# Two transfers of 64 rows for each output tile in place of one transfer over both batch halves

## The chip, the cores and the metric

The kernel runs on one core of a Trainium2 chip. The metric is the device time of one execution in microseconds (us); the time before is the median of three runs. A profile of one execution comes with it: for every instruction on every engine its start and duration, and for the 16 DMA engines of the core the packets that they moved. TensorE is PE in the rows, VectorE DVE, ScalarE ACT, GpSimd POOL and SyncE SP. "SPq" is the queue of SyncE, on which the transfers of this kernel are issued.

## What is computed

A decayed linear attention over 4 batches, 8 heads and 768 positions, then two feed-forward blocks without residuals over the 3072 tokens:

```python
for t in range(S):
    state = gamma[None, :, None, None] * state + np.einsum('bhd,bhe->bhde', k[:, :, t], v[:, :, t])
    y[:, :, t] = scale * np.einsum('bhd,bhde->bhe', q[:, :, t], state)
x = np.ascontiguousarray(y.transpose(0, 2, 1, 3)).reshape(B * S, H * D)   # 3072 x 512
# first block: 512 -> 1024 -> 512
h = x @ w_in; sm = softmax(h); solu = h * sm
x = (layernorm(solu) * g_ln) @ w_out
# second block: 512 -> 2048 -> 512
h = x @ w_in2
out = (h * np.cos(h)) @ w_out2
...
```

The output is 3072 x 512 in float32, with the rows ordered by batch and then by position.

## The kernel before

The attention works in 24 steps. A step takes 64 consecutive positions of two batches at once (`steps` holds pairs of batch pair `bp` and position block `i`), so the 128 rows that it yields are 64 rows of one batch followed by 64 rows of the next. The first feed-forward block follows on groups of two such steps, and its result goes to DRAM and comes back through `load_y`, for the second block.

The second block runs in six passes over 512 tokens (four steps of the attention each; the loop over `n` near the end of `body`). In each pass `up(n, j)` makes one of 16 slices of the hidden layer: 12 matmuls on PE (line 362), then the cosine and the split into a high and a low part on ACT and DVE. `down(n, j)` multiplies such a slice into four accumulators in PSUM, one for each tile of 128 tokens: 12 matmuls (line 387). `down` lags `up` by three slices. In the last pass the last three slices of `down` are run tile by tile, so that the four tiles end one after the other.

After the last slice of a tile, `down` copies the accumulator into a tile `o` in SBUF of 128 rows x 512 columns (four buffers), the left half on ACT and the right half on DVE (line 392), and issues the store to the output in DRAM on SP's queue (line 394). Row p of `o` belongs to batch `2*bp` for p below 64 and to batch `2*bp + 1` from 64 on. In DRAM the two halves lie 768 rows apart, and each of them is one unbroken stretch of 64 rows of 2 KB. The store before writes both halves in one transfer, whose target has three dimensions, 2 x 64 x 512:

```python
bp, i = steps[4 * n + t]
nc.sync.dma_start(
    out=out.rearrange("(p b s) f -> p b s f", b=2, s=S)[bp, :, i * C:(i + 1) * C], in_=o)
```

The order of PE's work is that of the program. The order on the other engines and on SP's queue is made by a planner from its own estimate of times. SP issues transfers in the order of its queue; before that, it waits for what the transfer needs. `load_y` for the next pass shares this queue: it reads four blocks of 128 x 512 (`yt`, line 350, two buffers), which ACT and DVE split into `yh` and `yl` (lines 120 and 123) for the next `up`. Other transfers that the prediction speaks of are in the attention's loads: `load_step` brings `X` and `W` in halves of 64 rows (lines 91, 92, 94 and 95, 128 KB each) and `kn` whole (line 96, 256 KB). `mm2` stores the first block's result in whole tiles of 128 rows (`y1d<-ys`, line 342, 256 KB). The program ends with waits of SP for the outstanding transfers and a barrier of all engines (line 629).

Of the kernel before, what the change touches and what calls it, by code (L numbers as in the profile page):

```python
# [21 lines left out]
B, H, S, D = 4, 8, 768, 64  # L22
C = 64
# [27 lines left out]
def body(ctx: ExitStack, tc: tile.TileContext, qx, kt, kn, vn, c_sc, c_mg,  # L51
         w_in1, w_out1, gln, w_in2, w_out2, out):
    nc = tc.nc
# [7 lines left out]

    y1d = [dram.tile([128, KD, 512], F32, name=f"y1d{n}") for n in range(NBLK)]

    # ---- phase 1 pools
    ph1 = ExitStack()
    p_w1 = ctx.enter_context(tc.tile_pool(name="w1", bufs=1, side="left", reuse_waits="tile"))
    p_u = ctx.enter_context(tc.tile_pool(name="u", bufs=2 * EARLY + 2, side="left", reuse_waits="tile"))
# [6 lines left out]
    pa = att.enter_context(tc.tile_pool(name="att", bufs=3, side="right", reuse_waits="tile"))  # L74
    psa = att.enter_context(tc.tile_pool(name="psa", bufs=1, side="right", space=PSUM))

    # ---- loads of a step of the attention
    steps = [(bp, i) for bp in range(NB2) for i in range(NI)]
    st = {}

# [30 lines left out]
    ident = const.tile([128, 128], F32, name="ident")  # L111
    make_identity(nc, ident)

    # ---- weights, each as a high and a low part
    w1h = p_w1.tile([128, KD, FF1], F32R, tag="w1h", name="w1h")
    w1l = p_w1.tile([128, KD, FF1], F32R, tag="w1l", name="w1l")
    o1 = []
# [87 lines left out]
        else:  # L205
            split(w2h[c][:, k], w2l[c][:, k], load_w(w_in2[k * 128:(k + 1) * 128, c * 1024:(c + 1) * 1024]))

    # ---- attention
    s_ps = [None]

    def att_prep(n):
# [49 lines left out]
            in1=d["mg"][:, 1].unsqueeze(2).to_broadcast([128, NHP, 2, C]), op=ALU.mult)  # L261
        xs[n] = x32

    # ---- first block
    lns = {}

    def split_x(n):
# [73 lines left out]
            nc.scalar.activation(out=ys, in_=y1, func=AF.Copy)  # L341
            nc.sync.dma_start(out=y1d[g // 2][:, 2 * p:2 * p + 2, (g % 2) * 256:(g % 2) * 256 + 256], in_=ys)

    # ---- second block
    def load_y(n):
        yh = p2["sb"].tile([128, KD, 512], F32R, tag="yh", name="yh")
        yl = p2["sb"].tile([128, KD, 512], F32R, tag="yl", name="yl")
        for k in range(KD):
            t = p2["sb"].tile([128, 512], F32, tag="yt", name="yt", bufs=2)
            nc.sync.dma_start(out=t, in_=y1d[n][:, k])  # L350
            split(yh[:, k], yl[:, k], t)
        p2["y", n] = (yh, yl)
# [25 lines left out]
    def down(n, j, tiles=range(4)):  # L378
        gh, gl = p2["g", n, j]
        wh, wl = p2["o", j]  # L380
        if ("acc", n) not in p2:
            p2["acc", n] = [p2["psacc"].tile([128, 512], F32, tag=f"acc{t}", name=f"acc{t}") for t in range(4)]
        for t in tiles:
            acc = p2["acc", n][t]
            ts_ = slice(t * 128, t * 128 + 128)
            for m, (a, w) in enumerate(((gh, wh), (gl, wh), (gh, wl))):
                nc.tensor.matmul(out=acc, lhsT=a[:, ts_], rhs=w, start=(j == 0 and m == 0),  # L387
                                 stop=(j == K2 - 1 and m == 2))
            if j == K2 - 1:
                o = p2["wo"].tile([128, DM], F32, tag="o", name="o", bufs=4)  # L390
                for c, eng in enumerate((nc.scalar.copy, nc.vector.tensor_copy)):
                    eng(o[:, c * 256:c * 256 + 256], acc[:, c * 256:c * 256 + 256])
                bp, i = steps[4 * n + t]
                nc.sync.dma_start(
                    out=out.rearrange("(p b s) f -> p b s f", b=2, s=S)[bp, :, i * C:(i + 1) * C], in_=o)

    def load_o2(g):
        if g < EARLY + 1:
# [6 lines left out]
        for e in range(2):  # L405
            p2["o", 2 * g + e] = (hi[:, e], lo[:, e])

    # ---- emission
    ns = len(steps)
    wq = [(load_w1, (k, c)) for c in range(2) for k in range(KD)] + [(load_o1, (j,)) for j in range(K1)]  # L410
    wq += [(load_w2, (p_w2a, 0, k)) for k in range(KD)]
# [144 lines left out]
    for n in range(NBLK):  # L556
        for j in range(LAG if n == 0 else 0, K2 + LAG):
            loads(1)
            if j < K2 and (n > 0 or j >= nup):
                up(n, j)  # L560
            if j == K2 and n + 1 < NBLK:
                load_y(n + 1)
            if j >= LAG and (n + 1 < NBLK or j <= K2):
                down(n, j - LAG)
    for t in range(4):
        for j in range(K2 - LAG + 1, K2):
            down(NBLK - 1, j, [t])
# [65 lines left out]
```

## Time and profile before

| | us |
|---|---|
| median of three runs | 967.81 |
| lowest and highest of them | 965.81, 970.95 |
| span of the profiled execution | 968.5 |
| PE busy in it | 916.3 (95%) |
| DVE busy | 622.7 (64%) |
| ACT busy | 452.6 (47%) |
| the second block's passes: matmuls of line 387 and of line 362, mean of one | 0.395, 0.394 |

The span runs from the first to the last instruction of one execution. A chain of waits follows the work back from the end: at each step to what released it. A view by windows gives, for a stretch of time, how long each engine was busy in it, the granted clock of TensorE as a share of full speed, the mean busy share of the 16 DMA engines and the GB/s that they moved. The duration of an SPq row is the time that the issue of the transfer held SP's queue, not the time until its data have landed.

### The profile page before, as it was taken

The page shows a single profiled execution, that of the slowest core. Times are in us where ns is not written, and L with a number is a line of the kernel's source. Part 1 is how long each engine was busy: PE and PEld are TensorE (multiplying, and loading weights), DVE is VectorE, ACT ScalarE, POOL GpSimd, SP SyncE. Part 2 cuts the span into 40 slices and gives each one's busy share as a digit, 9 for nine tenths or more (in the row PEclk, how much of TensorE's full clock was granted, in tenths as well). Part 3 has the DMA queues.
Part 4 walks back from the last instruction along what each step waited for, and adds up shares of the span by engine and source line. Part 5 has one row for each costly group of instructions (what it writes and reads, how often), then busy time and mean ns, then how long its engine had stood idle before and what let it go on. Part 6 is the DMA issues. An engine that isn't in the chain of part 4 may idle for free.

```text
span 968.5 us, 16031 instructions
## 1 busy us (share of the span) xinstructions
PE 916.3 (95%) x6464; PEld 774.9 (80%) x6464; DVE 622.7 (64%) x1090; ACT 452.6 (47%) x768; POOL 48.0 (5%) x60
## 2 busy tenths in 40 slices
PE   4787999999999999999999999999999999999991
PEld 4666899899898999988888888888888888888880
DVE  5799887668687654667657556555655575566550
ACT  4577766555665454544434334333433343343330
POOL 2112110111100100000000000000000000000000
PEclk7899999999999999999999999999999999999996
DMA  9996355647456231231010002001100100010001
GB/s 252 263 272 190 109 151 180 192 152 224 158 161 200 94 120 50 87 132 65 1 57 31 1 0 73 15 1 44 44 0 1 54 34 1 0 48 19 1 1 43
DMA packets 41163, 85.28 MB, mean 88 GB/s; under 512 B 4736, under 2 KB 11008, under 8 KB 41088
## 3 DMA queue, kind: packets, MB, share of 16 engines
q1 hardware_dynamic: 40656, 83.90, 27.9%
q8 instruction: 51, 0.84, 0.4%
q10 hardware_dynamic: 432, 0.34, 0.1%
q14 instruction: 24, 0.20, 0.1%
HBM read 64.30 MB, written 19.92 MB: 87 GB/s over the span
## 4 chain that ended last, share of the span: by engine, by line
PE 81%; DMA 6%; DVE 5%; ACT 3%; issue 2%; SPq 0%; POOL 0%; ACTq 0%; DVEq 0%
PE acc L387 28%; PE h L362 28%; PE y L337 12%; PE h L284 9%; DMA X<-qx_dram 2%; PE tr L320 2%; DMA kn<-kn_dram 2%; PE sc L224 1%; PE y L256 1%; PE S L244 1%; DVE X L227 1%; DVE wt L159 1%; ACT junk L297 1%; DMA raw<-w_in_dram 1%; ACT wt L153 1%
## 5 line engine op out<-in xcount | busy, mean ns | idle before, releaser
L387 PE MATMUL acc<-o2h,gl 128*128 128x512 f32 x384 | 151.9, 396 | 0.0
L387 PE MATMUL acc<-o2l,gh 128*128 128x512 f32 x384 | 151.7, 395 | 0.0
L362 PE MATMUL h<-yh,w2h 128*128 128x512 f32 x384 | 151.7, 395 | 0.0
L387 PE MATMUL acc<-o2h,gh 128*128 128x512 f32 x384 | 151.4, 394 | 0.0
L362 PE MATMUL h<-yl,w2h 128*128 128x512 f32 x384 | 151.4, 394 | 0.0
L362 PE MATMUL h<-yh,w2l 128*128 128x512 f32 x384 | 151.4, 394 | 0.0
L373 ACT ACTIVATE r<-r,hp 128x512 f32<-128x512 f32 x96 | 69.3, 722 | 144.6 <-DVE r L372 144.6
L370 DVE SCALAR_TENSOR_TENSOR r<-ki,h 128x512 f32<-128x512 int32 x96 | 65.9, 686 | 73.8 <-ACT ki L369 72.8
L337 PE MATMUL y<-lth,o1h 128*128 128x256 f32 x384 | 110.3, 287 | 0.0
L337 PE MATMUL y<-ltl,o1h 128*128 128x256 f32 x384 | 108.8, 283 | 0.0
L337 PE MATMUL y<-lth,o1l 128*128 128x256 f32 x384 | 108.6, 283 | 0.0
L374 DVE TENSOR_TENSOR r<-r,h 128x512 f32<-128x512 f32 x96 | 65.9, 687 | 61.6 <-ACT r L373 61.6
L369 ACT ACTIVATE ki<-h 128x512 int32<-128x512 f32 x96 | 57.2, 596 | 85.7 <-PE h L362 84.9
L123 DVE TENSOR_TENSOR gl<-r,gh 128x512 fp32r<-128x512 f32 x96 | 66.2, 690 | 45.9 <-ACT gh L120 45.4
L120 ACT ACTIVATE gh<-r 128x512 fp32r<-128x512 f32 x96 | 60.6, 632 | 65.4 <-DVE r L374 65.4
L387 PEld LDWEIGHTS acc<-o2h,gl 128*128 128x128 f32 x384 | 72.0, 187 | 17.8
L387 PEld LDWEIGHTS acc<-o2h,gh 128*128 128x128 f32 x384 | 72.0, 187 | 17.4
L387 PEld LDWEIGHTS acc<-o2l,gh 128*128 128x128 f32 x384 | 72.0, 188 | 17.3
L362 PEld LDWEIGHTS h<-yl,w2h 128*128 128x128 f32 x384 | 72.1, 188 | 17.0
L362 PEld LDWEIGHTS h<-yh,w2h 128*128 128x128 f32 x384 | 72.1, 188 | 17.0
L362 PEld LDWEIGHTS h<-yh,w2l 128*128 128x128 f32 x384 | 72.1, 188 | 16.6
L284 PE MATMUL h<-w1h,xh 128*128 128x512 f32 x192 | 78.1, 407 | 0.0
(79 smaller groups left out, 1594.0 us busy)
## 6 DMA issues: line engine op xcount, KB each, us to landing
raw<-w_in_dram SPq DMA_DIRECT2D x24, 512.0 KB
raw<-w_out_dram SPq DMA_DIRECT2D x24, 512.0 KB
kt<-kt_dram SPq DMA_DIRECT2D x24, 256.0 KB
X<-qx_dram SPq DMA_DIRECT2D x48, 128.0 KB
W<-vn_dram SPq DMA_DIRECT2D x48, 128.0 KB
kn<-kn_dram SPq DMA_DIRECT2D x24, 256.0 KB
y1d<-ys SPq DMA_DIRECT2D x24, 256.0 KB
yt<-y1d SPq DMA_DIRECT2D x24, 256.0 KB
```

The lines of the kernel that those rows point to most:

```text
L120: op = nc.scalar.activation(out=hi, in_=src if head is None else head, func=AF.Copy)
L123: nc.vector.tensor_tensor(out=lo, in0=src, in1=hi.bitcast(F32), op=ALU.subtract)
L153: first_op = nc.scalar.activation(out=f, in_=top.bitcast(F32), func=AF.Abs)
L284: nc.tensor.matmul(out=h[:, c], lhsT=a[:, k], rhs=w[:, k, cs], start=(k + m == 0), stop=(k == KD - 1 and m == 2))
L320: nc.tensor.transpose(out=tr[:, e, t * 128:(t + 1) * 128], in_=lns[2 * g + t].rearrange("p c f -> p (c f)")[:, j * 128:(j + 1) * 128], ide ...
L337: nc.tensor.matmul(out=y1[:, e], lhsT=w[:, j, ds], rhs=a[:, j % 2], start=(m == 0), stop=(m == 3 * K1 - 1))
L362: nc.tensor.matmul(out=h, lhsT=w[:, k, cs], rhs=a[:, k], start=(m == 0), stop=(m == 3 * KD - 1))
L369: nc.scalar.activation(out=ki, in_=h, func=AF.Identity, scale=INV2PI, bias=0.25)
L370: nc.vector.scalar_tensor_tensor(out=r, in0=ki, scalar=-C1, in1=h, op0=ALU.mult, op1=ALU.add)
L373: nc.scalar.activation(out=r, in_=r, func=AF.Sin, bias=p2["hp"])
L374: nc.vector.tensor_tensor(out=r, in0=r, in1=h, op=ALU.mult)
L387: nc.tensor.matmul(out=acc, lhsT=a[:, ts_], rhs=w, start=(j == 0 and m == 0), stop=(j == K2 - 1 and m == 2))
```

## The change

The store of an output tile becomes two, one for each half of 64 rows, both issued on SP's queue one after the other. What is stored, and where, stays the same. The other hunks of the diff touch comment lines alone.

```diff
                 bp, i = steps[4 * n + t]
-                nc.sync.dma_start(
-                    out=out.rearrange("(p b s) f -> p b s f", b=2, s=S)[bp, :, i * C:(i + 1) * C], in_=o)
+                for b in range(2):
+                    row = (2 * bp + b) * S + i * C
+                    nc.sync.dma_start(out=out[row:row + C], in_=o[b * C:(b + 1) * C])
```

## Rows read from the trace of the kernel before

**Rows 1.** The page: span, busy engines, DMA share in 40 slices.
```profile
span 968.5 us, 16031 instructions
PE 916.3 (95%) x6464; PEld 774.9 (80%) x6464; DVE 622.7 (64%) x1090; ACT 452.6 (47%) x768; POOL 48.0 (5%) x60
...
DMA  9996355647456231231010002001100100010001
```

**Rows 2.** Chain of waits, its last pieces: start us, us, what.
```profile
936.15 11.22 PE acc L387 x48
...
947.38 0.38 ACT o L392
...
947.79 0.42 DVE o L392
```

**Rows 3.** Windows of the end, columns in the first line.
```profile
core 0: us, PE busy (x) PEld busy (x) DVE busy (x) ACT busy (x) POOL busy (x), PEclk, DMA share, GB/s
...
948.21:950.00 1.79, 0.00 (x0) 0.00 (x0) 0.00 (x1) 0.00 (x0) 0.00 (x0) 1.00 0.13 48
950.00:967.00 17.00, 0.00 (x0) 0.00 (x0) 0.00 (x0) 0.00 (x0) 0.00 (x0) 0.55 0.13 51
967.00:967.20 0.20, 0.00 (x0) 0.00 (x0) 0.00 (x0) 0.00 (x0) 0.00 (x0) 0.50 0.08 31
967.20:967.80 0.60, 0.00 (x0) 0.00 (x0) 0.00 (x0) 0.00 (x0) 0.00 (x0) 0.50 0.00 0
967.80:968.50 0.70, 0.00 (x0) 0.00 (x0) 0.00 (x0) 0.00 (x0) 0.00 (x0) 0.50 0.00 0
```

**Rows 4.** Output stores: transfers in all, SP's issues at the end (start us, us), final wait.
```profile
out_dram<-o SPq DMA_DIRECT2D x24, 256.0 KB
...
944.03 1.91 SPq L394 DMA_DIRECT2D out_dram<-o  x2
...
945.43 0.51 SPq L394 DMA_DIRECT2D out_dram<-o  x1
...
948.24 5.98 SPq L394 DMA_DIRECT2D out_dram<-o  x1
...
SPq L629 <- DMA out_dram<-o: 13.3, 2, 8.2
```

**Rows 5.** SP's issues of a step's loads; last line: duration ns min/median/max of line 92.
```profile
296.94 0.33 SPq L96 DMA_DIRECT2D kn<-kn_dram  x1
298.01 0.47 SPq L91 DMA_DIRECT2D X<-qx_dram  x1
298.53 0.59 SPq L92 DMA_DIRECT2D X<-qx_dram  x1
299.17 0.59 SPq L94 DMA_DIRECT2D W<-vn_dram  x1
...
L92 SPq DMA_DIRECT2D X<-qx_dram x24: 471/588/1447, 1.8 to 298.5; - x24
```

**Rows 6.** A window in which the 64-row loads drain, columns as in rows 3.
```profile
300.50:302.00 1.50, 1.50 (x15) 1.50 (x14) 0.16 (x1) 0.80 (x2) 1.08 (x2) 1.00 0.67 212
```

**Rows 7.** A lone store of 128 rows: its issue, then windows as in rows 3.
```profile
332.16 0.37 SPq L342 DMA_DIRECT2D y1d<-ys  x1
...
332.16:332.90 0.74, 0.74 (x4) 0.58 (x4) 0.00 (x0) 0.74 (x1) 0.00 (x0) 1.00 0.00 0
...
333.20:333.90 0.70, 0.70 (x5) 0.58 (x4) 0.04 (x1) 0.70 (x3) 0.00 (x0) 1.00 0.99 309
```

**Rows 8.** Pass boundaries: a window after the first pass, timeline rows of a later one.
```profile
501.00:520.00 19.00, 19.00 (x85) 15.49 (x84) 13.69 (x24) 8.16 (x14) 0.00 (x0) 1.00 0.13 48
...
580.08 5.58 SPq L350 DMA_DIRECT2D yt<-y1d  x4
584.63 0.68 DVE L123 TENSOR_TENSOR yl<-yt,yh 128x512 fp32r<-128x512 f32 x1
588.89 9.72 SPq L394 DMA_DIRECT2D out_dram<-o  x4
...
590.09 10.92 PE h L362 x48
```

## Prediction

> **What bounds the kernel now.** I read the page first. PE is busy 916.3 of 968.5 us, and the slices show DMA at one tenth or less over most of the second half [rows 1]. So an edit to stores looks like one of no consequence, and through most of the kernel it is. The chain of waits says where to look instead: its last pieces are 48 matmuls, then ACT's and DVE's copies of the last tile, and it ends at 947.79 + 0.42 = 948.21 us [rows 2]. The span ends at 968.5. For 20.3 us no compute engine does anything, and the chain, which follows instructions, does not say why.
>
> The windows of that stretch do [rows 3]. From 950 to 967 all compute engines stand at zero while DMA moves 51 GB/s at a share of 0.13. Two of 16 engines are a share of 0.125. So the reader is to see two DMA engines working all the time and fourteen idle, at about 25.5 GB/s each. The amount fits: the four stores of the last pass are 4 x 256 KB = 1.05 MB [rows 4], and 1.05 MB at 51 GB/s is 20.6 us. The four are issued at 944.03, 945.43, (one tile later) and 948.24, a tile every 1.40 us, far quicker than 5.1 us for 256 KB at 51 GB/s. They pile up, and the last issue holds SP for 5.98 us [rows 4]. The last bytes move at about 967.12 (0.2 us at 31 instead of 51 GB/s is 0.12 us), then 0.68 us without traffic until 967.8, then 0.7 us of closing barrier [rows 3]. SP's wait at the end for the output's transfers, up to 8.2 us at once, is the same thing seen from the queue [rows 4]. The end of the kernel is bound by a transfer that runs on two engines of 16.
>
> A store of 128 rows with another form shows that the direction is not to blame: the 256 KB of y1d move at 309 GB/s with a share of 0.99 [rows 7].
>
> **The change, part by part.** Removed: 24 stores of 2 x 64 x 512. Added: 48 stores of 64 x 512, 128 KB each. What each form costs depends on how many DMA engines it gets. No store of 64 rows is in the trace; the nearest rows are the loads of X and W, which are 64 rows of 2 KB from one unbroken stretch of DRAM, issued on the same queue. The last of them drain from 300.5 to 302.0 at 212 GB/s and a share of 0.67 [rows 6]. The queue is first in, first out, the last whole load was issued at 296.94, before all four halves [rows 5], and the 318 KB of this window are less than the 512 KB of the four, so it is halves that I see there. A share of 0.67 cannot come from two engines, nor from eight (0.5).
>
> Issue on SP. The halves are issued 0.52 and 0.64 us apart [rows 5]; I take 0.64. A tile then costs SP 1.28 us, under the 1.40 us between tiles, so SP does not fall behind before the last tile. 24 more issues are some 15 us of SP's time in all, and SP waits most of the second block. The bound on the other side is the longest issue of line 92, 1.447 us [rows 5], taken while the queue was full of other loads.
>
> The tail, summed:
> - Issue of the last tile's first half: 948.24, as before, since PE, ACT and DVE are not touched [rows 2, 4].
> - Issue of the second half: + 0.64 = 948.88.
> - Issue to first bytes: the lone store is issued at 332.16 and nothing moves until 332.90 [rows 7]. I take 0.8: 949.68.
> - 128 KB at 212 GB/s [rows 6]: 0.62 us, 950.30. By 309 GB/s [rows 7] it would be 0.42.
> - Last byte to the end of the span: 0.68 + 0.70 = 1.38 as now [rows 3]: 951.7.
>
> The gain is 968.5 - 951.7 = 16.8 us. At the short end (0.52, 0.74, 0.42) the span is 951.3 and the gain 17.2. At the long end both issues of the last tile take 1.45 us: 948.24 + 1.50 + 1.45 + 0.43 + 0.62 + 1.38 = 953.6, gain 14.9 (0.43 is what is left of the 0.8 after an issue of 0.37 [rows 7]). I take the middle value because the queue is empty at the end, as it was for the lone store.
>
> The other five passes gain nothing, and I put that at zero. Their stores crawl the same way (share 0.13, 48 GB/s after the first pass), but PE is busy 19.00 of 19.00 us beside them [rows 8]. The o buffers are four and are needed again only a pass later. The cover is PE's work; it would be gone only if some load of the next pass waited in SP's queue behind the stores. The loads of yt are issued from 580.08, ahead of the stores at 588.89, and the last yl is ready at 585.31, before PE's next pass starts at 590.09 [rows 8].
>
> Two sentences of the Trainium skill bear on this. Its page "DMA: Bandwidth & Descriptors", section "Rules for kernel authors", speaks against the change: two transfers to disjoint partition halves are not worth it, since they serialize over the same 16 engines, and one transfer over 128 partitions is to be preferred. Its rule there on using all 16 engines speaks for it: an outermost dimension of size c below 16 confines the whole transfer to at most c engines, so the first rule compares with a 128-row form that this kernel does not have. The share of 0.13 agrees with the second.
>
> **The rivals.**
> 1. *The halves follow one another completely.* If the second half's first byte had to wait until the first half had landed, the sum would be 948.24 + 0.8 + 0.62 + 0.68 = 950.34 for the first and + 0.8 + 0.62 + 1.38 = 953.1 for the second: gain 15.4, time 952.4. Against it: 128 KB one after the other at 2.1 us each would be 62 GB/s, and the loads of X and W reach 212 [rows 6]. That first rule of the skill is of this kind.
> 2. *The new form does not get more engines either.* A store of one unbroken stretch may be handled otherwise than a load from one. Then the last 1.05 MB still leave at 51 GB/s, and nothing moves: 967.8. For it: no store of 64 rows is in the trace. Against it: the same shape on the load side [rows 6], and stores in general reach 309 GB/s [rows 7].
> 3. *Slower: the planner puts the stores ahead of a load.* 48 transfers in place of 24 change the planner's estimate, and it may queue the later loads of yt behind the eight half stores of a pass. The stores are ready from 588.89 and take 8 x 0.64 = 5.1 us to issue, so yt would go at 594.0 instead of 580.08 and yl be ready 5.2 us later (585.31 - 580.08), at 599.2. PE needs the third block of yl about six matmuls of 0.23 us into the pass, at 591.5 [rows 8]. PE would stand 7.7 us at each of five boundaries, 38 us, less 16.8: 989. It decides from 16.8 / 5 = 3.4 us per boundary. Against it: the loads go 8.8 us before the first store is ready, and nothing they wait for is changed.
>
> **How the numbers follow.** The forecast is 967.81 - 16.8 = 951.0; the profiled span stood 0.7 above the median, which I carry over as it is. Chances: the forecast 0.88, rival 1 0.04, rival 2 0.05, rival 3 0.03. A measurement of this kernel can tell about 0.5% (4.8 us) from no change. The forecast and rival 1 are faster by more than that: 0.92; rival 2 is the same: 0.05; rival 3 slower: 0.03. The range goes from the short end of the costs (967.81 - 17.2 = 950.6) to the long end (967.81 - 14.9 = 952.9). The three runs put the median within 2.0 of the lowest, so I widen by 2.0 on each side: 948.6 to 954.9. Rival 1 lies inside; rivals 2 and 3, with 0.08, are left out.
>
> **What would show it.** In the profile of the changed kernel the last DVE copy still ends near 948.2. SP's last issue starts near 948.9 and is short, around 0.6 us instead of 5.98. DMA has a share well above 0.5 for about half a microsecond for each half and is silent between tiles, where now it stands at 0.13 without a break; in the five earlier passes too, with PE as busy as before. From the last byte to the end it is still about 1.4 us. Wrong would be: a share of 0.13 and a tail of 20 us (rival 2), two bursts 2 us apart (rival 1), idle time of PE at the pass boundaries with DMA of yt as its releaser (rival 3), or issues of over 1.4 us, by which SP would become the limit of the tail.

## The result, and the profile after

The changed kernel takes 951.25 us (median of four runs, 950.22 to 952.07) against 968.0 for the kernel before (median of four): a ratio of 0.982, with a 95% interval of 0.9803 to 0.9837. The forecast was 951.0, with 948.6 to 954.9.

The page of the changed kernel: the span, the busy engines and the DMA share in 40 slices.

```profile
span 948.4 us, 16045 instructions
PE 917.0 (97%) x6464; PEld 776.5 (82%) x6464; DVE 622.4 (66%) x1090; ACT 452.8 (48%) x768; POOL 47.8 (5%) x60
...
DMA  9997355656456332242011003000300020001001
```

PE's busy time is what it was (916.3 in [rows 1]). The slices hide the change: DMA stands at one tenth in the last of them, as before. The chain of waits ends with the same pieces, and the windows behind it (columns as in [rows 3]) are where the time went:

```profile
932.43 11.22 PE acc L387 x48
...
943.67 0.38 ACT o L392
...
944.08 0.42 DVE o L392
```

```profile
core 0: us, PE busy (x) PEld busy (x) DVE busy (x) ACT busy (x) POOL busy (x), PEclk, DMA share, GB/s
941.40:947.00 5.60, 2.24 (x10) 1.48 (x8) 1.15 (x3) 0.74 (x2) 0.00 (x0) 0.91 0.80 189
...
944.50:945.20 0.70, 0.00 (x0) 0.00 (x0) 0.00 (x1) 0.00 (x0) 0.00 (x0) 1.00 0.86 202
945.20:947.00 1.80, 0.00 (x0) 0.00 (x0) 0.00 (x0) 0.00 (x0) 0.00 (x0) 0.72 0.78 181
947.00:947.70 0.70, 0.00 (x0) 0.00 (x0) 0.00 (x0) 0.00 (x0) 0.00 (x0) 0.50 0.00 0
947.70:948.40 0.70, 0.00 (x0) 0.00 (x0) 0.00 (x0) 0.00 (x0) 0.00 (x0) 0.50 0.00 0
```

The last DVE copy ends at 944.50 and the span at 948.4: a tail of 3.9 us, against 20.3 before [rows 2, 3]. In that stretch the stores move at 181 to 202 GB/s where they moved at 51, and the share is about 0.8 where it was 0.13. The 1.4 us behind the last byte are the same in both.

SP's queue at the end: the issue of the last tile's first half, the eight issues of the last pass (duration in ns, min/median/max), the stores' time from issue to landing (last column of the third line), and SP's waits that end the program (us in total, times, longest):

```profile
944.53 0.47 SPq L396 DMA_DIRECT2D out_dram<-o  x1
...
L396 SPq DMA_DIRECT2D out_dram<-o x8: 466/528/597, 940.3 to 945.0; - x8
...
out_dram<-o SPq DMA_DIRECT2D x48, 128.0 KB, 2.3
...
SPq L630 <- DMA out_dram<-o: 1.7, 2, 1.1
```

No issue of the last pass is held up any more: the longest takes 0.60 us, against 5.98 in [rows 4]. The waits at the end fell from 13.3 to 1.7 us in total.

How each tile's bytes follow its issue is read from the first and the last of the four tiles. The first is issued at 940.32, with nothing ahead of it in the queue:

```profile
940.32 1.11 SPq L396 DMA_DIRECT2D out_dram<-o  x2
...
941.20:941.40 0.20, 0.20 (x3) 0.15 (x2) 0.13 (x1) 0.04 (x1) 0.00 (x0) 1.00 0.00 0
941.40:941.60 0.20, 0.20 (x2) 0.16 (x1) 0.20 (x1) 0.00 (x0) 0.00 (x0) 1.00 0.63 164
...
941.40:945.60 4.20, 2.24 (x10) 1.48 (x8) 1.15 (x3) 0.74 (x2) 0.00 (x0) 1.00 0.81 189
945.60:947.00 1.40, 0.00 (x0) 0.00 (x0) 0.00 (x0) 0.00 (x0) 0.00 (x0) 0.64 0.80 187
```

Its first bytes move from 941.4, some 1.1 us after the issue. By 945.6 DMA has moved 4.20 us x 189 GB/s = 794 KB, which is the first three tiles (3 x 262 KB = 786 KB). So the bytes of the last tile, issued at 944.53, begin at about 945.6, again 1.1 us after the issue, and take 1.4 us.

The two profiles differ by 20.1 us in span, but the tail accounts for only 16.4 of it. The other 3.7 lie before the last 48 matmuls: these start at 932.43 here and at 936.15 in [rows 2]. Experiment 10 shows that this belongs to the single execution and not to the change.

### The profile page after: what moved, and what is told of

Same layout as the page of the kernel before. It is cut to its first block, busy times and chain, and to the rows that moved or that the text cites. A ratio compares the mean times of both kernels' runs of the same rounds, so it can differ in the third digit from the quotient of the medians.

```text
span 948.4 us, 16045 instructions
## 1 busy us (share of the span) xinstructions
PE 917.0 (97%) x6464; PEld 776.5 (82%) x6464; DVE 622.4 (66%) x1090; ACT 452.8 (48%) x768; POOL 47.8 (5%) x60
## 4 chain that ended last, share of the span: by engine, by line
PE 90%; DMA 4%; DVE 2%; ACT 2%; issue 1%; SPq 0%; POOL 0%; ACTq 0%; DVEq 0%
PE acc L387 28%; PE h L362 28%; PE y L337 14%; PE h L284 11%; DMA kn<-kn_dram 3%; PE tr L320 2%; PE y L256 2%; PE sc L224 2%; PE S L244 1%; DMA W<-vn_dram 1%; DVE X L227 1%; ACT kn L218 1%; DMA mg<-c_mg_dram 0%; PE S L242 0%; PE sc L225 0%
## 5 line engine op out<-in xcount | busy, mean ns | idle before, releaser
L362 PEld LDWEIGHTS h<-yh,w2l 128*128 128x128 f32 x384 | 72.2, 188 | 16.6
```

Of the source, the lines that this page charges most:

```text
L362: nc.tensor.matmul(out=h, lhsT=w[:, k, cs], rhs=a[:, k], start=(m == 0), stop=(m == 3 * KD - 1))
```

## The experiments

The tail below is always the time from the end of the last DVE copy to the end of the span. The diffs are against the changed kernel.

**1 and 2. Which stores count.** Half stores in the last pass alone, then in the other five alone.

```diff
+                if n == NBLK - 1:        # the second kernel: n < NBLK - 1
                     for b in range(2):
                         row = (2 * bp + b) * S + i * C
                         nc.sync.dma_start(out=out[row:row + C], in_=o[b * C:(b + 1) * C])
+                else:
+                    nc.sync.dma_start(
+                        out=out.rearrange("(p b s) f -> p b s f", b=2, s=S)[bp, :, i * C:(i + 1) * C], in_=o)
```

> Two half stores in the last pass alone (n = 5), the one store of before in the first five. My theory: only the stores behind the last matmul are on the path, so the whole gain is here: about 951 us, and a tail (end of the last DVE copy to the end of the span) of 3.9 us as in the changed kernel, against 20.3 before; DMA at a share of 0.13 after each of the first five passes, with PE busy all the time. Rival (the earlier stores cost time too, by holding SP's queue or the o buffers): less gain than the change has, above 953 us.

> The reverse: half stores in the first five passes, the one store of before in the last. My theory: no gain, 968 us, with a tail of 20.3 us. Rival (the earlier stores cost time too): 955 to 966 us, by what the first run lacks.

Last pass alone: 952.04 us, ratio 0.9842 (0.9825 to 0.9858), a tail of 949.1 - 945.27 = 3.8 us. First five alone: 967.56 us, ratio 1.0001 (0.9986 to 1.0016), a tail of 967.0 - 946.76 = 20.2 us. A window after the first pass of the former, and a window in the tail of the latter:

```profile
500.00:515.00 15.00, 15.00 (x67) 12.29 (x66) 11.25 (x19) 7.48 (x13) 0.00 (x0) 1.00 0.13 50
```

```profile
950.00:965.00 15.00, 0.00 (x0) 0.00 (x0) 0.00 (x0) 0.00 (x0) 0.00 (x0) 0.50 0.13 51
```

Both rows show the slow store at a share of 0.13. In the first PE is busy beside it for all of the 15 us and nothing is lost; in the second nothing else runs. The gain is in the last pass, within what the times can tell.

**3. A whole tile in one transfer of 128 rows.** The target is one unbroken stretch, so the rows of the output stand in another order than the reference's.

```diff
-                for b in range(2):
-                    row = (2 * bp + b) * S + i * C
-                    nc.sync.dma_start(out=out[row:row + C], in_=o[b * C:(b + 1) * C])
+                row = (4 * n + t) * 128
+                nc.sync.dma_start(out=out[row:row + 128], in_=o)
```

> One store of 128 unbroken rows of the output for each tile (256 KB), so that the rows of the output are in another order than the reference's. What the halves cost against a whole is to be seen. My theory (64 rows reach only part of what moves them, so halves run at 200 GB/s and a whole one at the 309 GB/s of the store of y1d): bursts of 0.9 us near 300 GB/s with silence between tiles, a tail of 3.1 to 3.4 us, 950.6 us. Rival (a store of unbroken output rows runs at 200 GB/s whatever its rows in SBUF): 200 GB/s nearly without a break, a tail of 3.7 to 4 us.

950.56 us, ratio 0.9821 (0.9802 to 0.9839), a tail of 948.9 - 945.81 = 3.1 us. The last issue and the windows behind it:

```profile
945.85 0.33 SPq L395 DMA_DIRECT2D out_dram<-o  x1
```

```profile
946.60:947.40 0.80, 0.00 (x0) 0.00 (x0) 0.00 (x0) 0.00 (x0) 0.00 (x0) 0.71 0.84 328
947.40:948.90 1.50, 0.00 (x0) 0.00 (x0) 0.00 (x0) 0.00 (x0) 0.00 (x0) 0.50 0.00 0
```

256 KB in 0.8 us at 328 GB/s, where the two halves took some 1.4 us at 187. The first bytes come about 0.8 us after the issue (945.85 to 946.65), where those of a half take 1.1. The halves cost 0.8 us of tail against a whole. The unbroken target is not what limits them.

**4 and 5. The size of the outermost dimension.** One transfer per tile with four stretches of 32 rows, then eight of 16; here too the rows of the output are in another order.

```diff
+                g, q = 4, 32             # the second kernel: g, q = 8, 16
+                nc.sync.dma_start(
+                    out=out.rearrange("(g s) f -> g s f", g=g)[:, (4 * n + t) * q:(4 * n + t + 1) * q], in_=o)
```

> One store of 256 KB for each tile with 4 stretches of 32 rows as its outermost dimension, 768 rows apart, so that the rows of the output are in another order than the reference's. My theory (the size of the outermost dimension is the number of DMA engines): share 0.25, 4 x 25.5 = 102 GB/s, 1.05 MB in 10.3 us, a tail of 8.5 us, 956 us. Rival (any target in several stretches runs on two engines): share 0.13, tail 20.3 us, 968 us. Rival (only a size of 2 is slow): tail under 4 us.

> One store of 256 KB for each tile with 8 stretches of 16 rows as its outermost dimension, 384 rows apart (another order of the output's rows than the reference's). My theory (outermost size is the number of engines): share 0.5 while a tile drains, 8 x 25.5 = 204 GB/s, 1.28 us for a tile, just under the 1.40 us between tiles, so no pile and a tail of 3.5 to 4 us, 951 us. Rival (two engines, or another number): 20.3 us of tail, or in between.

Four: 958.84 us, ratio 0.9903 (0.9884 to 0.9922), tail 957.6 - 947.04 = 10.6 us. Eight: 954.03 us, ratio 0.9878 (0.9841 to 0.9916), tail 949.1 - 942.88 = 6.2 us. The stretches in which they drain, the first two rows of four, the last of eight:

```profile
943.60:946.20 2.60, 2.57 (x12) 1.72 (x10) 0.85 (x2) 0.56 (x2) 0.00 (x0) 1.00 0.20 25
946.20:955.60 9.40, 0.00 (x0) 0.00 (x0) 0.42 (x1) 0.37 (x1) 0.00 (x0) 0.68 0.26 101
```

```profile
939.80:947.50 7.70, 2.22 (x10) 1.46 (x8) 1.13 (x3) 0.75 (x2) 0.00 (x0) 0.97 0.48 135
```

The shares are 0.26 and 0.48, that is four and eight engines of 16, after 0.13 for two: the number of busy engines, as the share gives it, is the size of the outermost dimension. Both rivals (two engines for any target in stretches; only a size of two slow) fall. The Trainium skill has the rule, on the page "DMA: Bandwidth & Descriptors", section "Rules for kernel authors": an outermost dimension of size c below 16 confines the transfer to at most c engines. These rows agree with it.

My tails were too short, 8.5 and 3.5 to 4, because I gave every engine 25.5 GB/s from the start. Four engines moved 25 GB/s together for the first 2.6 us and 101 only then; eight came to 135 on average, not 204. The kernel before has such a slow start too. Its two engines moved 28 GB/s at the same share of 0.13 before they reached 51 [rows 3]:

```profile
945.00:947.35 2.35, 2.35 (x11) 1.54 (x9) 0.83 (x2) 0.37 (x1) 0.00 (x0) 1.00 0.13 28
```

Why, no run here settles. The times of the kernel with eight stretches lie from 951.0 to 957.7 us, more widely than those of the others, and its profile is of the fastest.

**6. Where the 64 rows lie.** Both stores take the tile's middle rows; the outer 64 rows are not stored.

```diff
-                    nc.sync.dma_start(out=out[row:row + C], in_=o[b * C:(b + 1) * C])
+                    nc.sync.dma_start(out=out[row:row + C], in_=o[32:96])
```

> As the change, but both half stores take the tile's rows 32 to 95 (the other rows of the tile are not stored), with the same number, size and targets. My theory (the rate of a 64-row store hangs on where its rows lie in SBUF; rows 0 to 63 or 64 to 127 reach half of the ways into it, rows 32 to 95 reach all of them): bursts at 280 to 310 GB/s with silence between tiles, a tail of 3.2 to 3.5 us. Rival (the size of 128 KB or the unbroken target sets the rate): 200 GB/s at a share of 0.87 as in the changed kernel, a tail of 3.9 us.

952.37 us, ratio 0.9842 (0.9807 to 0.9877), a tail of 950.7 - 946.96 = 3.7 us. Windows of 0.2 us at about the same DMA share: a half store of the changed kernel, then three of this one.

```profile
945.00:945.20 0.20, 0.00 (x0) 0.00 (x0) 0.00 (x0) 0.00 (x0) 0.00 (x0) 1.00 0.97 225
```

```profile
948.60:948.80 0.20, 0.00 (x0) 0.00 (x0) 0.00 (x0) 0.00 (x0) 0.00 (x0) 1.00 0.01 0
948.80:949.00 0.20, 0.00 (x0) 0.00 (x0) 0.00 (x0) 0.00 (x0) 0.00 (x0) 1.00 0.96 379
949.00:949.20 0.20, 0.00 (x0) 0.00 (x0) 0.00 (x0) 0.00 (x0) 0.00 (x0) 1.00 0.74 277
```

The same count, size and targets, with all engines busy: 379 against 225 GB/s, and silence between the bursts. So the rate of a 64-row store hangs on which rows of SBUF it takes, not on its size. The Trainium skill, page "SBUF — State Buffer", section "Door 1: The DMA port swizzle (why `[64,N]` ≈ `[32,N]`)", says that rows 0 to 63 reach the 8 even ports of 16 and rows 64 to 127 the odd ones, and gives 196 GB/s for 64 rows in a transfer of 1 MiB. The rates of the halves (181 to 202) and of rows 32 to 95, which reach both sides by that table, agree.

The tail shrank by only 0.2 us, less than I expected (a tail of 3.2 to 3.5 us): what is left is mostly the time from issue to bytes. The first half of the last tile is issued at 946.99, 0.03 us after the copy, and the bytes of the second begin only at 948.8.

**7 and 8. The second half on ACT's queue.** In every pass, then in the last alone.

```diff
-                for b in range(2):
+                for b, eng in enumerate((nc.sync, nc.scalar)):   # 8: nc.scalar if n == NBLK - 1 else nc.sync
                     row = (2 * bp + b) * S + i * C
-                    nc.sync.dma_start(out=out[row:row + C], in_=o[b * C:(b + 1) * C])
+                    eng.dma_start(out=out[row:row + C], in_=o[b * C:(b + 1) * C])
```

> As the change, but the second half of each tile is issued on ACT's queue, so that both halves are in flight at once and neither waits for the other's issue. If halves of two queues add up in rate: bursts near 300 GB/s, the last bytes 0.5 us from the issue of the other half, a tail of 3.2 us, 950.6 us. If they share one rate of 200 GB/s (they serialize): a tail of 3.4 to 3.9 us at 200 GB/s. If ACT's issues (0.5 us each) delay its next copy: the copies stand over 1.40 us apart. None of these can be told by time alone (0.1%); the profile's windows tell them.

> The second half of each tile on ACT's queue in the last pass alone; on SP's in the first five. My theory of the run with two queues in every pass: PE stood some 2.1 us at each of five pass boundaries, because the planner ordered ACT's and DVE's work otherwise once ACT issues transfers there; the two queues themselves cost nothing. Then PE is busy all the time at the boundaries here, the time is that of the change, 951 us, and the tail 3.7 us as with two queues in every pass. Rival (a queue of ACT beside one of SP costs time at any place, or in the last pass): above 954 us or a tail over 4 us.

In every pass: 965.77 us, ratio 0.9977 (0.9961 to 0.9993). Nearly the whole gain was gone, which none of my lines foresaw, though the tail is 962.5 - 958.79 = 3.7 us. The window over the first pass boundary in the changed kernel, then in this one, and this one's waits of PE from 480 to 930 us:

```profile
480.00:520.00 40.00, 40.00 (x175) 32.41 (x174) 25.74 (x45) 17.41 (x30) 0.00 (x0) 1.00 0.19 53
```

```profile
480.00:520.00 40.00, 37.93 (x157) 30.35 (x156) 24.23 (x42) 15.71 (x27) 0.00 (x0) 0.96 0.17 53
...
PE h L362 <- DVE r L374: 10.6, 5, 2.4
```

PE stands still at each of the five boundaries, 10.6 us in all, waiting for a step of the cosine. At two of them, the first and the last, the idle time is followed by a granted clock of 0.50, the lower of its two levels (1.2 GHz of 2.4); at the other three, as long, it is not. The windows around the first:

```profile
504.00:506.30 2.30, 0.23 (x2) 0.00 (x0) 1.49 (x5) 1.83 (x4) 0.00 (x0) 0.99 0.00 0
506.30:508.00 1.70, 1.70 (x4) 1.41 (x5) 1.61 (x3) 1.22 (x2) 0.00 (x0) 0.50 0.02 5
...
506.31 4.56 PE h L362 x12
```

The 12 matmuls of the last row (chain of waits) take 4.56 us where 12 at full clock take 2.80; at the last boundary it is 4.61. That is 1.76 + 1.81 = 3.6 us, and 10.6 + 3.6 = 14.2 us in this execution is nearly what separates the medians: 965.77 - 951.25 = 14.5.

ACT's rows there (timeline, the second boundary) show an order that the changed kernel does not have. `ki`, line 369, is the first step of the cosine, three steps `r` on DVE (lines 370 to 372) follow it, and the sine on ACT is line 373:

```profile
592.05 0.60 ACT L369 ACTIVATE ki<-h 128x512 int32<-128x512 f32 x1 [1.86 <-PE h L362]
594.77 0.60 ACT L369 ACTIVATE ki<-h 128x512 int32<-128x512 f32 x1 [2.12 <-PE h L362]
597.83 0.60 ACT L369 ACTIVATE ki<-h 128x512 int32<-128x512 f32 x1 [2.45 <-DVE r L372]
598.32 1.32 ACT L373 ACTIVATE r<-r,hp 128x512 f32<-128x512 f32 x2
```

Three `ki` stand before the first sine, and the third waits for DVE. In the changed kernel the first sine comes after two, at 592.45 when the second `ki` starts at 591.96:

```profile
589.24 0.60 ACT L369 ACTIVATE ki<-h 128x512 int32<-128x512 f32 x1 [2.45 <-PE h L362]
591.96 0.60 ACT L369 ACTIVATE ki<-h 128x512 int32<-128x512 f32 x1 [2.12 <-PE h L362]
592.45 0.71 ACT L373 ACTIVATE r<-r,hp 128x512 f32<-128x512 f32 x1
```

With the second queue in the last pass alone, PE is busy 40.00 of 40 us at every boundary and the time is 951.18 us, ratio 0.9819 (0.9801 to 0.9836). So it is the issues on ACT in the first five passes that cost the time. That they do it through the order that the planner then gives ACT and DVE, and not by the 0.5 us of each issue, is read from rows and was not tested by a run of its own. ACT's last issue at the second boundary ends at 591.01 + 0.80 = 591.81, before the first `ki`, and the first two `ki` are as far apart as in the changed kernel, 2.72 us. But DVE, after the first `r` step of the first slice, stands for 2.03 us until the second `ki` is there; in the changed kernel it goes straight on with the first slice (last row):

```profile
591.01 0.80 ACTq L396 DMA_DIRECT2D out_dram<-o  x1
...
595.40 0.69 DVE L370 SCALAR_TENSOR_TENSOR r<-ki,h 128x512 f32<-128x512 int32 x1 [2.03 <-ACT ki L369]
596.01 1.29 DVE L371 SCALAR_TENSOR_TENSOR r<-ki,r 128x512 f32<-128x512 int32 x2
```

```profile
590.59 0.69 DVE L371 SCALAR_TENSOR_TENSOR r<-ki,r 128x512 f32<-128x512 int32 x1
```

The second queue does not help the tail either: 947.5 - 943.11 = 4.4 us. The rival had named a tail over 4 us, and in the tail it was right. Its last tile drains in two rows; below them are the last tile of experiment 7 and 0.2 us out of it:

```profile
944.10:945.30 1.20, 0.00 (x0) 0.00 (x0) 0.00 (x0) 0.00 (x0) 0.00 (x0) 1.00 0.77 208
945.30:946.00 0.70, 0.00 (x0) 0.00 (x0) 0.00 (x0) 0.00 (x0) 0.00 (x0) 0.62 0.05 18
```

```profile
959.80:961.00 1.20, 0.00 (x0) 0.00 (x0) 0.00 (x0) 0.00 (x0) 0.00 (x0) 0.68 0.78 219
960.60:960.80 0.20, 0.00 (x0) 0.00 (x0) 0.00 (x0) 0.00 (x0) 0.00 (x0) 0.50 1.13 420
```

Over a whole tile two halves in flight from two queues move at 208 to 219 GB/s, a little above the 187 of one queue, and in experiment 8 a remainder at a share of 0.05 trailed for another 0.7 us. The last tile of experiment 7 has no such remainder; one execution each says no more. The mean hides that the rate is not even: for 0.2 us it reaches 420 GB/s, which no window of 0.2 us in the changed kernel's tail does. So the halves add up for a moment; why only then is open. The Trainium skill, page "SBUF — State Buffer", section "Can I just issue two DMAs to hit both halves?", says no, with 6% gained. The means here agree that little is gained, but it is 11 to 17%, and the 420 GB/s do not fit its statement that the two serialize.

**9. Tiles of one batch.** The rows of the output in the reference's order, and whole tiles all the same: the tokens are regrouped where the first block's second product reads its moving operand.

```diff
-lhsT=w[:, j, ds], rhs=a[:, j % 2], ...
+lhsT=w[:, j, ds], rhs=a[:, j % 2].rearrange("p (t b s) -> p b t s", t=2, b=2), ...
...
+                bp, i = steps[4 * n + t // 2 * 2]
+                row = (2 * bp + t % 2) * S + i * C
+                nc.sync.dma_start(out=out[row:row + 128], in_=o)
```

> The tokens of each group of two attention steps are put in the order batch, step, position by the view in which the second matmul of the first block reads its moving operand, so that an output tile holds 128 positions of one batch and leaves in one store of 256 KB to one unbroken stretch, with the reference's order of rows. If the moving operand's view costs PE nothing: as with one transfer of 128 rows, bursts near 400 GB/s, a tail of 3.1 us, 0.8 less than the change, 950.5 us, and SP issues 24 stores. Rival: the view slows the 1152 matmuls of the first block's second product, 283 to 287 ns before; 10 ns each are 11.5 us, 962 us.

951.65 us, ratio 0.983 (0.9816 to 0.9843), a tail of 948.9 - 945.80 = 3.1 us. The last tile's burst, and a group of the matmuls with the new view:

```profile
946.60:947.40 0.80, 0.00 (x0) 0.00 (x0) 0.00 (x0) 0.00 (x0) 0.00 (x0) 1.00 0.84 328
...
L337 PE MATMUL y<-lth,o1h 128*128 128x256 f32 x384 | 110.3, 287 | 0.0
```

The view costs PE nothing (287 ns as in the kernel before) and the tail is the 3.1 us of experiment 3. In time this cannot be told from the change: 0.8 us is under a tenth of a per cent.

**10. The change again**, on the chip of experiments 8 and 9, unedited.

> The changed kernel once more, beside the two others on one chip. Both theories: 951 us and a tail of 3.9 us. The stretch before the last pass's first matmul, 3.7 us shorter in the changed kernel's profile than in that of before, is a matter of the single execution if it comes out otherwise here; if it belongs to the change, it is 3.7 us shorter again.

951.65 us, ratio 0.9822 (0.9802 to 0.9842). The profiled span is 951.6, and the last copy ends at 947.22 + 0.42 = 947.64, which leaves a tail of 4.0 us:

```profile
947.22 0.42 DVE o L392
```

That copy ended at 944.50 in the first profile of the same kernel and at 948.21 in that of before. What lies before the last 48 matmuls varies by 3.1 us from one execution of this kernel to the other, and in the second the last copy ends within 0.6 us of that in the kernel before.

## Why the prediction was right, step by step

- *What bounds the end.* Right, and by rows: two engines of 16 drained 1.05 MB for 20 us behind the last matmul. Experiments 4 and 5 show that the two is the outermost dimension, and 1 and 2 that it matters only in the last pass.
- *The other five passes at zero.* Right: 1.0001 for half stores there alone.
- *The gain of 16.8 us.* The tail lost 20.3 - 3.9 = 16.4, and the medians lost 967.81 - 951.25 = 16.6. That 951.0 is only 0.25 us off is partly luck: the tail was 0.4 us longer than the sum's 951.7 - 948.21 = 3.5, and the four runs lie 1.9 us apart.
- *Term by term.* Second issue: 0.52 measured for the 0.64 that I took. Last byte to the end: 1.4 for 1.38. The middle was too small: from the first issue of the last tile to the last byte I had 0.64 + 0.8 + 0.62 = 2.06 us, and it took 947.0 - 944.53 = 2.5. Two terms were too small. The larger miss is the 0.8 us from issue to first bytes, read from a store of 128 rows: a half took 1.1 us. The other is the rate: from the first bytes to the last the two halves took 1.4 us at 187 GB/s, where the sum leaves them 0.64 + 0.62 = 1.26. That the queue would be empty was right: the third tile was still draining at 944.50, but its bytes were through when those of the last began, and these came no later after their issue than those of the first tile. Why a half starts later than a whole, no run here settles; rows 32 to 95 do so too (experiment 6: issued at 946.99, first bytes after 948.0).
- *Silence between tiles.* Wrong: DMA stood at a mean share of 0.80 from 941.4 to 947.0. I had the rate in [rows 6] and the pitch in [rows 4] and did not divide one by the other: 256 KB at 212 GB/s is 1.24 us of 1.40, with hardly a gap, and at the 187 measured it is all of the 1.40.
- *From span to median.* I took 968.5 for 0.7 above the median. Spans of the changed kernel stand 1.7 to 1.8 below their own times, so the profiled execution of before was one of the longer ones. It did no harm, because only a difference inside one trace was carried to the median.
- *Rival 1, halves one after the other.* It would have had a second burst 2 us after the first; the bursts join. *Rival 2, no more engines:* the share of 0.8 refutes it. *Rival 3, the planner:* in the changed kernel ACT and DVE have the order of before all through the second block, and PE is busy 40.00 of 40 us at the first boundary. A relative of it is real all the same: in experiment 7, by its rows, another order on ACT and DVE, not a late load of yt, cost 14 us.

## What to carry to other kernels

When a span goes on after the last compute instruction, read the DMA share there: a steady 0.13 is two engines of 16, and the outermost dimension of the transfer says why. Give a transfer that nothing covers an outermost dimension well above the 2, 4 and 8 that were slow here (64 and 128 were not), rows from all of the tile's 128 if its target allows that, and leave covered transfers alone. An edit of this kind belongs on the queue that has it already: moved to an engine that computes, it can reorder that engine's work.

## What was not expected of the hardware

A stand of PE of 2 us can cost more than itself: behind two of five such stands the granted clock was 0.50 and the next 12 matmuls took 1.8 us longer. The rate of 64 rows depends on which rows they are: 225 GB/s for an outer half and 379 for rows 32 to 95, at the same share of busy DMA engines (0.97 and 0.96). The first bytes of a store of 64 rows come 1.1 us after its issue, those of 128 rows 0.8. And engines do not always have their 25 GB/s: four of them moved 25 GB/s together for 2.6 us before they reached 101, and eight averaged 135; the cause is open.
